# A linear attention block gated by a mixer MLP: the first step of each scale chain and its negations on VectorE instead of GpSimd, and a new table of due times

## The chip, the cores and the metric

The kernel runs on one core of one Trainium2 chip. The metric is the device time of one execution in microseconds (us), taken as the median of several runs. TensorE, VectorE, ScalarE and GpSimd are called PE, DVE, ACT and POOL, as in the profile; PEld is the loading of weights into PE, which overlaps the matmuls, and SP issues most of the DMAs.

## The reference

All data are fp32, with S = 2048 rows, D = 512 columns, 32 heads of 16, and F = 1376.

```python
xn = layernorm(x)
q, k, v = split_heads(xn @ wqkv)
phi = lambda t: where(t > 0, t + 1, exp(t)) + 1e-6
kv = einsum("bhsd,bhse->bhde", phi(k), v)
z = einsum("bhsd->bhd", phi(k))
o = (phi(q) @ kv) / (phi(q) . z + 1e-6)
s = merge_heads(o) @ wo
h = gelu(layernorm(xn) @ w1)
x1 = xn + shift_rows_by_column_quarter(h) @ w2
h2 = gelu(layernorm(x1) @ w3) @ w4
out = x + s * silu(x1 + h2)
```

The attention has no mask, so `kv` and `z` are sums over all rows.

## The kernel before

The 2048 rows are cut into 16 tiles of 128 rows, and four of these make a block; there are four blocks. Names carry the tile or the block as a number: `x5` is a tile of rows, `kr2` the key of tile 2. A product in fp32 is made of three fp32r products: an operand is split into a rounded part (`h` at the end of its name) and a rest (`l`), the rounding on ACT, the subtraction on DVE (`rounded`). A group of three matmuls on the same operands shows as `hh`, `lh`, `hl` in the trace.

The work runs in stages. First come keys and queries from the rows, and with each finished tile of keys a gram matrix `g` of rows and keys (tiles `k`, `q`, `g`; `gram`, `query`, `key`); from block 1 on, pairs of tiles are made together with fewer products (`pair_kq`, tiles `pax`, `pbx`, `pex`). Then come the mixer's first matmul (`h`), its second (`seven`, tiles `pam`, `pbm`, `pem`), the up projection (`a`, `pa`, `pb`, `pe`) with attention between (`pas`, `pbs`, `pes`), and the down projection (`acc`, `pbd`, `ped`).

`pair_kq` and `seven` are alike. Each makes seven products for four results, and uses a PSUM bank more than once: a product is added up in the bank, ACT copies the sum out (`p1`, `p5`, `u2`) or DVE adds it to such a copy (`o`, `so`, `h_a220f`), and then further matmuls add to what still stands in the bank (`go(..., False)`). The first of these must wait until the copy has read the bank. PE can meanwhile work on other products, where the order puts some.

Statistics of the rows are made on ACT, by a sum and a sum of squares (`totals`, tile `sq` into `mv`), or on DVE (`moments`). Three functions turn them into scales. `scale_x` makes, for one to four tiles, `w` (variance times a constant plus epsilon), its power −1/2 (`rs`, function `power`), the negated scale `ns`, and from these `nm` and `mr`; `halves_x` then scales and splits the rows. `spread` does the first two steps for a block (`pu`, then `an`), and PE transposes `an` into a row (`ab`). `mixed` does it for the second layer norm (`w2`, `rs2`, `nm2`). Before the change all these small steps are on POOL, which also computes the power and issues the accumulating DMAs (`gather`).

Nothing in this order is fixed by hand. The functions only add operations to a plan, in program order, each with an engine, a duration and its operands. `Plan.emit` then orders every engine's operations: PE goes by a nominal sequence, every other operation gets a due time back from those that need it, and the one due first among the ready ones is issued. A table `SOONER` shifts due times: of each pair of numbers in it, the first names an operation by its place in the plan, and the second moves its due time ahead by that many quarters of a microsecond:

```python
for n, k in zip(table[::2], table[1::2]):
    self.ops[n].due -= .25 * k
self.backward()
```

The result is one instruction stream for each engine, in which an instruction that waits holds everything behind it.

Of the kernel before, what the change touches and what calls it, by code (L numbers as in the profile page):

```python
# [11 lines left out]
ALU = mybir.AluOpType  # L12
# [3 lines left out]
EPS = 1e-5  # L16
# [380 lines left out]
def linear_attn_gated_by_mixer(  # L397
# [20 lines left out]
    QT = 4  # L418
# [16 lines left out]
    KV = KM * KM / D  # L435
# [10 lines left out]
    pl = Plan(nc, pools, counts, ("acc", "mm"))  # L446
# [14 lines left out]
    def fixed(name, n, dt=F32):  # L461

        t = pl.new("const", name, dt, n)
        t.ap = const.tile([P, n], dt, name=name)
        return t
# [37 lines left out]
    mv1, mv2 = fixed("mv1", 2 * NT), fixed("mv2", 2 * NT)  # L503
# [24 lines left out]
    def var(mv, a, b):  # L528
        return mv.cut([(2 * i + 1, 2 * i + 2) for i in range(a, b)], b - a,
                      lambda ap: ap.rearrange("p (t k) -> p t k", k=2)[:, a:b, 1])  # L530
# [48 lines left out]
    def small(name, n):  # L579
        return pl.new("sm", name, F32, n)  # L580
# [17 lines left out]
    def scale_x(lo, n):  # L598

        r, s, m = (v[:, lo:lo + n] for v in (rs1, ns1, nm1))  # L600
        w = small(f"w{lo}", n).all
        km, kv = (1.0, 1.0) if QT <= lo < 2 * QT else (KM, KV)
        pl.ts(w, var(mv1, lo, lo + n), kv, EPS, ALU.mult, ALU.add, eng="POOL")
        power(r, w, n)
        pl.ts(s, r, -km if lo < QT else -1.0, None, ALU.mult, eng="POOL")
        pl.tt(m, means(mv1, lo, lo + n), s, ALU.mult, eng="POOL")
        if lo < QT:
            pl.ts(mr1[:, lo:lo + n], m, -1.0, None, ALU.mult, eng="POOL")
        elif km != 1.0:
            pl.ts(m, m, km, None, ALU.mult, eng="POOL")  # L610
        for i in range(lo, lo + n):
            halves_x(i)

    def spread(b):

        u, m = (an[:, (2 * b + k) * QT:(2 * b + k + 1) * QT] for k in range(2))
        p = small(f"pu{b}", QT).all
        km, kv = (1.0, 1.0) if b == 1 else (KM, KV)
        pl.ts(p, var(mv1, b * QT, b * QT + QT), kv * (1.0 + EPS), EPS * EPS, ALU.mult, ALU.add, eng="POOL")
        pl.ts(m, means(mv1, b * QT, b * QT + QT), -km, None, ALU.mult, eng="POOL")  # L620
        power(u, p, QT)
        ps = pl.new("mm", f"ab{b}", F32, 512)[:2 * QT, :P]
        pl.transpose(ps, an[:, 2 * b * QT:2 * (b + 1) * QT], ident.all)
        t = pl.new("p", f"ar{b}", F32, PIECE)[:2 * QT, :P]
        pl.act(t, ps, AF.Copy)
        for k, row in enumerate((arow, nrow)):
            dst = row[:, EDGE + b * BT:EDGE + (b + 1) * BT]
            pl.store(dst.via(lambda ap: ap.rearrange("o (j p) -> (o j) p", p=P)),
                     t.via(lambda ap, k=k: ap[k * QT:(k + 1) * QT]))
# [391 lines left out]
    def mixed(i, xv):  # L1021

        b, j = divmod(i, QT)
# [6 lines left out]
        a, z = i - QT + 1, i + 1  # L1030
        r, m = rs2[:, a:z], nm2[:, a:z]
        w = small(f"w2{b}", QT).all
        pl.ts(w, var(mv2, a, z), KV, EPS, ALU.mult, ALU.add, eng="POOL")
        power(r, w, QT)
        pl.tt(m, means(mv2, a, z), r, ALU.mult, eng="POOL")
        pl.ts(m, m, -KM, None, ALU.mult, eng="POOL")
# [627 lines left out]
    b = 2  # L1664
# [21 lines left out]
    b = 3  # L1686
# [72 lines left out]
    for b in LATE:  # L1759
# [5 lines left out]
        down_late(b, final)  # L1765

    SOONER = (
# [42 lines left out]
    )  # L1810
    pl.emit(first=6.0, lead={"p": 9.0, "w": 20.0, "ab": 10.0}, reserve={"p": 8, "w": 1, "ab": 0}, window=9.0,
            ahead=6.0, table=SOONER)
# [39 lines left out]
```

## Time and profile before

| | us |
|---|---|
| runs | 503.18, 502.1, 502.8 |
| median | 502.8 |
| profiled execution | 502.62 |
| its span | 500.9 |
| first matmul starts | 1.04 |
| last matmul starts | 496.33 |

The granted clock of PE is 1.00 over the whole span. In the rows of a timeline stand the start in us from the beginning of the span, the duration in us, the engine, the line of the program (often that of a helper), the operation, what it writes and reads, and, in brackets, how long the engine stood idle ahead of it and what ended the wait. Ends of matmuls are modelled, so what is read from them is the distance between starts. In the groups of a view by lines stand the busy time of the group, the mean of one in ns, and then the idle time of the engine before them.

### The profile page before, as it was taken

What the parts mean: (1) busy time and instruction counts of PE and PEld (TensorE: products, weight loads), DVE (VectorE), ACT (ScalarE), POOL (GpSimd) and SP (SyncE); (2) the same over time, 40 slices, a digit from 0 to 9 for tenths busy, and PEclk for the clock granted to TensorE, in tenths of its full rate; (3) what the DMA queues carried; (4) which work ended last, traced back from release to release, by engine and by line L of the source; (5) the groups of instructions that cost most, each with busy time, mean ns of one, the idle gap of its engine ahead of it and who ended that gap; (6) DMA issues with size and microseconds to landing.
All of it is one profiled execution on the core that took longest, in us unless ns stands there. A gap on an engine that the chain in (4) does not pass through costs nothing.

```text
span 500.9 us, 9569 instructions
## 1 busy us (share of the span) xinstructions
PE 495.3 (99%) x3138; PEld 442.8 (88%) x3138; DVE 430.1 (86%) x850; ACT 368.0 (73%) x826; POOL 119.2 (24%) x208
## 2 busy tenths in 40 slices
PE   9999999999999999999999999999999999999996
PEld 6788778888888897899999989999989999999996
DVE  5998888789999958999899999978899785787983
ACT  5898999968696589999977855554657676856631
POOL 1384504438930232133100022000013100000320
PEclk9999999999999999999999999999999999999999
DMA  7968994999975899989978779975648937974674
GB/s 220 328 167 233 224 289 128 214 347 284 343 201 133 221 272 276 277 200 273 371 231 220 235 214 200 303 225 178 203 145 145 283 124 246 294 225 135 117 195 131
DMA packets 84345, 113.35 MB, mean 226 GB/s; under 512 B 10024, under 2 KB 37960, under 8 KB 84296
## 3 DMA queue, kind: packets, MB, share of 16 engines
q1 hardware_dynamic: 73640, 93.35, 57.2%
q0 software_dynamic: 10656, 19.40, 23.5%
q8 instruction: 24, 0.39, 0.3%
q14 instruction: 25, 0.20, 0.1%
HBM read 72.47 MB, written 36.06 MB: 217 GB/s over the span
## 4 chain that ended last, share of the span: by engine, by line
PE 94%; ACT 3%; DMA 1%; SPq 0%; DVE 0%; issue 0%; ACTq 0%
PE acc L146 12%; PE pb L146 11%; PE g L146 9%; PE h L146 9%; PE pbd L146 6%; PE pe L146 6%; PE pbx L146 5%; PE pbs L146 5%; PE pbm L146 5%; PE ped L146 3%; PE pa L146 3%; PE pex L146 3%; PE q L146 3%; PE pem L146 2%; PE pes L146 2%; PE a L146 2%
## 5 line engine op out<-in xcount | busy, mean ns | idle before, releaser
L225 POOL DMA_DIRECT2D xo<-x1d x12 | 10.6, 1067 | 186.7 <-DVE qz L201 112.6
L225 POOL DMA_DIRECT2D o<-xnd x16 | 14.0, 885 | 39.7 <-DMA w_s<-in_w 11.9
L225 POOL DMA_DIRECT2D zacc<-ke x12 | 12.3, 1028 | 31.9 <-DVE u_2l L191 9.9
L225 POOL DMA_DIRECT2D th<-in_x x14 | 12.1, 878 | 32.0 <-DVE th L201 14.3
L168 ACT ACTIVATE th<-xo 128x512 f32<-128x512 f32 (+1 forms) x16 | 9.7, 614 | 11.1 <-DVE xo L201 10.3
L225 POOL DMA_DIRECT2D xt<-nrow x16 | 15.1, 1441 | 6.0 <-DVE wt_01l L191 3.5
L191 DVE TENSOR_TENSOR ht<-h,abc 128x512 f32<-128x512 f32 x16 | 11.1, 691 | 5.6 <-PE h L146 5.4
L168 ACT ACTIVATE ht<-ht 128x512 f32<-128x512 f32 x16 | 9.9, 628 | 4.2 <-DVE ht L191 4.0
L168 ACT ACTIVATE p<-pe 128x256 f32<-128x256 f32 x20 | 7.6, 382 | 7.2 <-PE pe L146 7.1
L168 ACT ACTIVATE p<-pb 128x256 f32<-128x256 f32 x20 | 7.7, 383 | 7.2 <-PE pb L146 7.1
L196 POOL TENSOR_SCALAR w<-mv 128x4 f32<-128x4 f32 (+2 forms) x10 | 2.9, 289 | 40.0 <-ACT sq L168 39.7
L168 ACT ACTIVATE y<-o,nm,rs 128x512 f32<-128x512 f32 x16 | 12.0, 806 | 0.5 <-POOL nm L196 0.5
L168 ACT ACTIVATE u<-pb 128x256 f32<-128x256 f32 x20 | 7.7, 383 | 5.9 <-PE pb L146 5.8
L201 DVE SCALAR_TENSOR_TENSOR th<-th,so 128x512 f32<-128x512 f32 (+1 forms) x17 | 11.1, 652 | 0.8 <-ACT th L168 0.4
L168 ACT ACTIVATE sq<-o,mv 128x512 f32<-128x512 f32 x16 | 11.4, 719 | 0.1
L201 DVE SCALAR_TENSOR_TENSOR pq<-pq,rd 128x512 f32<-128x512 f32 x16 | 10.9, 682 | 0.3
L168 ACT ACTIVATE den<-den 128x32 f32<-128x32 f32 x16 | 3.6, 228 | 9.8 <-DVE den L1421 9.8
L201 DVE SCALAR_TENSOR_TENSOR qz<-pq,zb 128x512 f32<-128x512 f32 x16 | 10.8, 680 | 0.0
L168 ACT ACTIVATE gf<-gf 128x256 f32<-128x256 f32 (+1 forms) x20 | 10.5, 523 | 0.3
L1421 DVE TENSOR_REDUCE den<-qz 128x32 f32<-128x512 f32 x16 | 10.7, 676 | 0.1
L168 ACT ACTIVATE sq<-o 128x512 f32<-128x512 f32 x16 | 10.1, 630 | 0.1
L596 POOL TENSOR_TENSOR rs<-w,nhalf 128x4 f32<-128x4 f32 (+2 forms) x10 | 9.6, 962 | 0.7
(1974 smaller groups left out, 2383.5 us busy)
## 6 DMA issues: line engine op xcount, KB each, us to landing
w_s<-in_w SPq DMA_DIRECT2D x28, 256.0 KB, 5.8
x<-in_x SPq DMA_DIRECT2D x16, 256.0 KB, 5.1
xt<-in_xt SPq DMA_DIRECT2D x16, 256.0 KB, 5.7
xnd<-x SPq DMA_DIRECT2D x16, 256.0 KB, 6.0
xt<-nrow POOLq DMA_DIRECT2D x16, 256.0 KB, 8.2
pqd<-qr SPq DMA_DIRECT2D x16, 256.0 KB, 3.3
o<-xnd POOLq DMA_DIRECT2D x16, 256.0 KB, 6.0
x1d<-o SPq DMA_DIRECT2D x16, 256.0 KB, 5.8
```

The source lines that it names most:

```text
L146: lambda: nc.tensor.matmul(out.get(), lhs.get(), rhs.get(), start=start, stop=stop, skip_group_check=more))
L168: nc.scalar.activation(out.get(), src.get(), func, scale=get(scale), **kw)
L191: self.vec(eng, out, [a, b], lambda: self.e(eng).tensor_tensor(out.get(), a.get(), b.get(), op=op), True)
L196: lambda: self.e(eng).tensor_scalar(out.get(), a.get(), get(s1), get(s2), **kw), False,
L201: lambda: self.nc.vector.scalar_tensor_tensor(out.get(), a.get(), get(s), b.get(), op0=op0, op1=op1),
L225: lambda: self.nc.gpsimd.dma_start(out.get(), get(src), accum_op=ALU.add), mb=mb)
L596: lambda: g.tensor_tensor(out.get(), src.get(), nh.get(), op=ALU.pow))
L1421: pl.add("DVE", .6, .68, [t], [den], lambda: nc.vector.tensor_reduce(den.get(), t.get().rearrange("p (h d) -> p h d", d=DH), axis=AX.X, op ...
```

## The change

Four calls lose their `eng="POOL"`, so that DVE executes them: `w` and `ns` in `scale_x` (six of each), `pu` in `spread` (four) and `w` in `mixed` (four), twenty instructions in all. The power and the steps that follow from it stay on POOL.

```diff
@@ scale_x
-        pl.ts(w, var(mv1, lo, lo + n), kv, EPS, ALU.mult, ALU.add, eng="POOL")
+        pl.ts(w, var(mv1, lo, lo + n), kv, EPS, ALU.mult, ALU.add)
         power(r, w, n)
-        pl.ts(s, r, -km if lo < QT else -1.0, None, ALU.mult, eng="POOL")
+        pl.ts(s, r, -km if lo < QT else -1.0, None, ALU.mult)
@@ spread
-        pl.ts(p, var(mv1, b * QT, b * QT + QT), kv * (1.0 + EPS), EPS * EPS, ALU.mult, ALU.add, eng="POOL")
+        pl.ts(p, var(mv1, b * QT, b * QT + QT), kv * (1.0 + EPS), EPS * EPS, ALU.mult, ALU.add)
@@ mixed
-        pl.ts(w, var(mv2, a, z), KV, EPS, ALU.mult, ALU.add, eng="POOL")
+        pl.ts(w, var(mv2, a, z), KV, EPS, ALU.mult, ALU.add)
@@ the table of due times
     SOONER = (
-        15, 27, 20, 21, 26, 2, 30, 3, 36, 10, 52, 1, 82, 2, 91, 2, 99, 4, 103, 12, 112, -14, 113, -2, 124, 10,
...
+        10, 31, 24, 16, 26, 19, 28, 6, 72, 6, 91, 2, 95, 6, 97, 47, 100, 39, 117, 4, 124, 10, 133, 4, 138, 15,
...
     )
```

The table is replaced by a longer one, so the order of every engine is another. The matmuls are the same, and so are the DMAs. Three places follow; the number at the end of a name is that of a buffer.

PE, in `pair_kq` of block 1 at 58 us of the profile, from the last matmul into the bank `pex` ahead of its copy to the first behind it. Before:

```order
L146 MATMUL pex_788<-kq_t11h,xs_0l 128x512
L146 MATMUL pbx_719<-kq_t21h,xs_1h 128x512
L146 MATMUL pbx_719<-kq_t21l,xs_1h 128x512
L146 MATMUL pbx_719<-kq_t21h,xs_1l 128x512
L146 MATMUL pex_788<-wq_2h,xs_3h 128x512
L146 MATMUL pex_788<-wq_2l,xs_3h 128x512
```

Now (the last matmul into `pex` ahead of the copy, of `kq_t11h` and `xs_0l`, stands two rows ahead of these):

```order
L146 MATMUL pax_797<-wk_2l,u_2h 128x512
L146 MATMUL pax_797<-wk_2h,u_2l 128x512
L146 MATMUL pax_797<-wk_3h,u_3h 128x512
L146 MATMUL pax_797<-wk_3l,u_3h 128x512
L146 MATMUL pax_797<-wk_3h,u_3l 128x512
L146 MATMUL pbx_756<-kq_t20h,xs_1h 128x512
L146 MATMUL pbx_756<-kq_t20l,xs_1h 128x512
L146 MATMUL pbx_756<-kq_t20h,xs_1l 128x512
L146 MATMUL pbx_756<-kq_t21h,xs_1h 128x512
L146 MATMUL pbx_756<-kq_t21l,xs_1h 128x512
L146 MATMUL pbx_756<-kq_t21h,xs_1l 128x512
L146 MATMUL pex_779<-wq_2h,xs_3h 128x512
```

Where the three matmuls of one `pbx` group stood between the two, a whole `pax` group of six and two `pbx` groups stand now.

PE in the up projection at 388 us, from the last matmul into the bank `pb_1` ahead of DVE's `h_a220f` to the first behind it. Before (that last one, of `yt32h` and `w_1_s1l`, stands just ahead):

```order
L146 MATMUL pas_5536<-m_b21h,q12h 128x256
L146 MATMUL pas_5536<-m_b21l,q12h 128x256
L146 MATMUL pas_5536<-m_b21h,q12l 128x256
L146 MATMUL pas_5536<-m_b21h,q12h 128x256
L146 MATMUL pas_5536<-m_b21l,q12h 128x256
L146 MATMUL pas_5536<-m_b21h,q12l 128x256
L146 MATMUL pb_1_5429<-yt42h,w_1_b 128x256
```

Now:

```order
L146 MATMUL pb_1_5444<-yt32h,w_1_s1l 128x256
L146 MATMUL pas_5526<-m_b21l,q12h 128x256
L146 MATMUL pas_5526<-m_b21h,q12l 128x256
L146 MATMUL pas_5526<-m_b21h,q12h 128x256
L146 MATMUL pas_5526<-m_b21l,q12h 128x256
L146 MATMUL pe_1_5461<-yb222h,w_1_s1l 128x256
L146 MATMUL pe_1_5461<-yb222h,w_1_s1h 128x256
L146 MATMUL pe_1_5461<-yb222l,w_1_s1h 128x256
L146 MATMUL pe_1_5461<-yb222h,w_1_s1l 128x256
L146 MATMUL pas_5526<-m_b21h,q12l 128x256
L146 MATMUL pb_1_5444<-yt42h,w_1_b 128x256
```

The six matmuls into `pas` are five, with four into `pe_1` among them.

DVE at 22 to 26 us, where the scales of tiles 1 to 3 are made (`kt` is a step of the keys, `BN_STATS` a statistic of block 1, `wq_0l` and its like the rests of weights). Before:

```order
L201 SCALAR_TENSOR_TENSOR kt_320<-wneg,mv_90,k_145 128x512
L191 TENSOR_TENSOR wq_0l<-wq_s_157,wq_0h 128x512
L201 SCALAR_TENSOR_TENSOR kt_335<-wneg,mv_90,k_147 128x512
L191 TENSOR_TENSOR wq_3l<-wq_s_176,wq_3h 128x512
L191 TENSOR_TENSOR wq_1l<-wq_s_153,wq_1h 128x512
L201 SCALAR_TENSOR_TENSOR kt_358<-wneg,mv_90,k_165 128x512
L584 BN_STATS st_369<-x_234 128x6
L584 BN_STATS st_374<-x_240 128x6
L584 BN_STATS st_382<-x_254 128x6
L584 BN_STATS st_392<-x_264 128x6
```

Now:

```order
L201 SCALAR_TENSOR_TENSOR kt_320<-wneg,mv_90,k_155 128x512
L201 SCALAR_TENSOR_TENSOR kt_327<-wneg,mv_90,k_145 128x512
L191 TENSOR_TENSOR wq_0l<-wq_s_160,wq_0h 128x512
L196 TENSOR_SCALAR w_343<-mv_90 128x2
L584 BN_STATS st_346<-x_210 128x6
L196 TENSOR_SCALAR w_355<-mv_90 128x1
L191 TENSOR_TENSOR wq_2l<-wq_s_173,wq_2h 128x512
L196 TENSOR_SCALAR ns_94<-rs_92 128x2
L201 SCALAR_TENSOR_TENSOR kt_366<-wneg,mv_90,k_165 128x512
L196 TENSOR_SCALAR ns_94<-rs_92 128x1
L196 TENSOR_SCALAR x_197<-x_197,rs_92,nm_95 128x512
```

The two `w` and the two `ns` stand among the corrections `kt` and the rests of the weights, and three of the four statistics have gone further back.

99 rows, old and new, of the table SOONER are left out of this document.

## The prediction

> **What bounds the kernel now.** I read the page first, then the table of stretches, then the list of what the weight loads wait for, then the rows around each hole that this list names.
>
> From the page (busy time and share of each engine; the chain that ended last):
>
> ```profile
> PE 495.3 (99%) x3138; PEld 442.8 (88%) x3138; DVE 430.1 (86%) x850; ACT 368.0 (73%) x826; POOL 119.2 (24%) x208
> PE 94%; ACT 3%; DMA 1%; SPq 0%; DVE 0%; issue 0%; ACTq 0%
> ```
>
> From the view by stretches (PE, PEld, DVE, ACT, POOL busy, then the granted clock):
>
> ```profile
> 60.00:70.00 10.00, 10.00 (x45) 8.00 (x44) 8.17 (x16) 10.00 (x19) 1.10 (x2) 1.00 1.02 243
> 495.00:501.00 6.00, 1.61 (x14) 1.41 (x12) 2.58 (x6) 0.73 (x2) 0.00 (x0) 1.00 0.24 87
> ```
>
> TensorE sets the end: 94% of the chain, at full clock. POOL, which loses work, is busy for 24% of the span and absent from the chain; DVE, which gains it, is at 86%. So neither the relief of POOL nor the load on DVE is the question. It is whether TensorE has holes, and whether the new order closes or opens some. The page's 99% hides them, because a waiting matmul is drawn longer.
>
> A hole shows in the distance from one start to the next. Timeline around 58 us:
>
> ```profile
> 57.76 0.39 PE L146 MATMUL pex<-kq_t11h,xs_0l 128*128 128x512 f32 x1
> 58.19 0.69 ACT L168 ACTIVATE p5x<-pex,ns 128x512 f32<-128x512 f32 x1
> 58.23 0.39 PE L146 MATMUL pbx<-kq_t21l,xs_1h 128*128 128x512 f32 x1
> 58.46 0.40 PE L146 MATMUL pbx<-kq_t21h,xs_1l 128*128 128x512 f32 x1
> 58.93 0.50 PE L146 MATMUL pex<-wq_2h,xs_3h 128*128 128x512 f32 x1
> 59.27 0.39 PE L146 MATMUL pex<-wq_2l,xs_3h 128*128 128x512 f32 x1
> ```
>
> Unhindered, 512-column matmuls start every 0.23 us (58.23 to 58.46). Here two steps are 0.47 and 0.34, so 0.24 + 0.11 = 0.35 us is lost. The reason is a bank that is used again: the matmul at 58.93 adds into the bank that ACT is still copying to p5x, which it began after the matmul of 57.76 and ended at 58.88. Only three matmuls (0.70 us) stand between, against 0.69 of copy. I call this a loop: last matmul into a bank, copy, next matmul into the bank; its cover is the TensorE work put between. I measured the excess over 0.23 (512 columns) and 0.117 (256) of every step: about 2.4 us in all behind the first matmuls, of which some 0.6 at the very start and the larger rest in a few loops. **No order can gain more than about 2.4 us**, and the change leaves every matmul in.
>
> **The change part by part.** *The loops whose cover grows.* Beside the one above (3 matmuls before, 12 after: −0.35) these are it. Weight loads in the m products that waited, and the first of their holes:
>
> ```profile
> 191.13 0.19 PEld L146 LDWEIGHTS pbm<-w_t2h,hs21h 128*128 128x128 f32 x1 [0.44 <-ACT p1m L168]
> 193.40 0.19 PEld L146 LDWEIGHTS pbm<-w_t3h,hs31h 128*128 128x128 f32 x1 [0.45 <-ACT u2m L168]
> 195.01 0.19 PEld L146 LDWEIGHTS pbm<-w_t4h,ha221h 128*128 128x128 f32 x1 [0.48 <-DVE o L191]
> 191.13 0.50 PE L146 MATMUL pbm<-w_t2h,hs21h 128*128 128x256 f32 x1
> 191.47 0.28 PE L146 MATMUL pbm<-w_t2l,hs21h 128*128 128x256 f32 x1
> 191.59 0.28 PE L146 MATMUL pbm<-w_t2h,hs21l 128*128 128x256 f32 x1
> ```
>
> 191.13 to 191.47 is 0.34, where 191.47 to 191.59 is 0.12: 0.22 lost. The other two, stepped the same way, lose 0.22 and 0.18. Cover less copy was 0.47, 0.47 and 0.43 us there; in the new order it is 0.64, 2.00 and 0.66. Together −0.62.
>
> ```profile
> 216.28 0.27 PE L146 MATMUL pbm<-w_t3h,hs32l 128*128 128x256 f32 x1
> 216.52 0.39 PE L146 MATMUL pem<-w_b22h,hs42h 128*128 128x256 f32 x1
> 216.75 0.28 PE L146 MATMUL pem<-w_b22l,hs42h 128*128 128x256 f32 x1
> ...
> 217.34 0.36 PE L146 MATMUL pbm<-w_t4h,ha222h 128*128 128x256 f32 x1
> 217.54 0.28 PE L146 MATMUL pbm<-w_t4l,ha222h 128*128 128x256 f32 x1
> ```
>
> Two steps of 0.24 and 0.23 for 0.12 each (0.23 lost), and 0.20 at 217.34 (0.08). These two loops go from 6 to 10 and from 6 to 8 matmuls of cover: −0.31.
>
> ```profile
> 354.18 0.28 PE L146 MATMUL pb<-yb111h,w_ah 128*128 128x256 f32 x1
> 354.43 0.19 PEld L146 LDWEIGHTS pbs<-m_t4h,q 128*128 128x128 f32 x1 [0.18 <-DVE so L191]
> 354.65 0.28 PE L146 MATMUL pbs<-m_t4l,q 128*128 128x256 f32 x1
> ...
> 387.12 0.28 PE L146 MATMUL pb<-yt32h,w_s1l 128*128 128x256 f32 x1
> 387.66 0.42 DVE L191 TENSOR_TENSOR h_a220f<-pb,p 128x256 f32<-128x256 f32 x1
> 387.83 0.28 PE L146 MATMUL pas<-m_b21h,q12l 128*128 128x256 f32 x1
> 388.14 0.38 PE L146 MATMUL pb<-yt42h,w_b 128*128 128x256 f32 x1
> 388.36 0.28 PE L146 MATMUL pb<-yt42l,w_b 128*128 128x256 f32 x1
> ```
>
> At 354 two steps lose 0.24, and one matmul more (7 to 8) gives 0.12, just the 0.13 of its first step: −0.24, to 0 if that tenth does not do. At 388 the steps 387.83 to 388.14 to 388.36 are 0.31 and 0.22: 0.29 lost. Here DVE frees the bank, late; cover goes from 6 matmuls to 9, three steps or 0.35 us more: −0.29. Sum of the gains: 0.35 + 0.62 + 0.31 + 0.24 + 0.29 = **1.81 us**.
>
> *The loops whose cover shrinks.* With matmul counts times 0.117 and the copies' own durations of before, cover less copy falls in pbm, w_t4h with ha222h (one product earlier than at 217), from 0.68 to 0.32; in pem, w_b22h with hs43h, from 0.68 to 0.33; in pb, w_s1h with yt32h, from 0.32 to 0.20. What 0.32 costs, the old rows tell twice: 0.23 at 216.52, and 0.03 here (383.09 less 382.94 less 0.12):
>
> ```profile
> 382.94 0.31 PE L146 MATMUL pb<-yt32h,w_s1h 128*128 128x256 f32 x1
> 383.09 0.28 PE L146 MATMUL pb<-yt32l,w_s1h 128*128 128x256 f32 x1
> ```
>
> I take the middle, 0.13, for each of the first two, and 0.15 for the third (0.12 less cover than in these rows): **+0.41**, between 0.1 and 0.7.
>
> *The first gram.* The new order puts k2h behind three cq and an ar on ACT, and in front of k3h:
>
> ```profile
> 31.61 0.62 ACT L168 ACTIVATE k2h<-kr 128x512 fp32r<-128x512 f32 x1
> 32.39 0.27 ACT L168 ACTIVATE ar<-ab 8x128 f32<-8x128 f32 x1 [0.16 <-PE ab L151]
> 32.56 1.93 ACT L168 ACTIVATE cq<-qneg,mr 128x512 f32<-128x512 f32 x3
> ```
>
> k2h moves later by 1.93 + 0.27 − 0.62 = 1.6 us less what ACT did sooner (wait before ar 0.16, rounding of wq moved), to an end near 33.5; counted in steps, TensorE wants it at 33.35. The first product of x1h and k1h is asked for eight places earlier than before, and is about as close. I take **+0.3** for both, between 0 and 0.6. The first loads are issued in another order too (two pieces of xt ahead of a piece of wk); **+0.1** for that, between −0.5 and +0.5, the size of the holes at the start.
>
> *The twenty moved instructions.* On POOL they are these (and `w` shapes of one and two columns at about the same price); the nearest DVE operation is the BATCH_NORM_AGGREGATE, of a two-column output:
>
> ```profile
> L196 POOL TENSOR_SCALAR w<-mv 128x4 f32<-128x4 f32 x7 | 1.8, 258 | 27.7 <-ACT sq L168 27.4
> L196 POOL TENSOR_SCALAR ns<-rs 128x4 f32<-128x4 f32 x3 | 3.4, 1122 | 0.1
> 28.54 0.38 DVE L585 BATCH_NORM_AGGREGATE mv<-st 128x2 f32<-128x6 f32 x4
> 24.02 1.26 POOL L596 TENSOR_TENSOR rs<-w,nhalf 128x2 f32<-128x2 f32 x2
> ```
>
> Four aggregates fill 0.38, so 0.10 each is the floor; POOL's 0.26 is the ceiling. Twenty make 1.9 to 5.2 us of DVE in 501, and I take the floor, as it is DVE's own row. None lies on the chain: DVE has 14% free. I cost them at nothing. Without that cover each would cost its 0.1 to 0.26 once, in a stretch where ACT and TensorE have no slack (60 to 70 above). What could cost more is waiting: DVE works in order, `w` waits for ACT's square sums and `ns` for POOL's power in the last row, 1.26 for two. The new order puts a statistic or a weight rounding between `w` and `ns`, which I take as cover enough: 0.
>
> [...]
>
> *Sum.* −1.81 + 0.41 + 0.3 + 0.1 + 0 = −1.0. Against the profiled execution's 502.62 (span 500.9 and 1.7 around it) that is **501.6**; the median of the runs shown is 502.8, 0.2 above, so 501.8 by that. The tail after the last matmul (the 495 to 501 row: TensorE 1.61 of 6.00) keeps its operations, and I cost it at nothing, up to +0.1. I forecast 501.7.
>
> **The rivals.** A measurement of this kernel tells about 0.2%, 1.0 us, from no change.
>
> *The moved waits eat the gain.* Around 24 us DVE stands at `ns` until POOL's two powers are through: 1.26, and behind it are the k products' corrections, which the first gram waits for. Then −1.81 + 0.41 + 0.3 + 0.1 + 1.26 = +0.3, **502.9**: no change. For it: ACT's rows from 31.61 on leave no more than 0.16 between its operations. Against: before, POOL did the whole chain in its own time, and DVE still waits for nothing more than it did, if the operation between is long enough (0.6). [...]
>
> *Thin loops break in numbers: slower.* The new order still has 46 loops with under 0.5 us of cover less copy (before: 52, of which eight, at 0.2 each, made 1.6 of the 1.81). Whether such a loop stalls depends on one operation of DVE or ACT, 0.4 to 0.7 us in the rows above, standing in front of the copy, as at 387.66, where DVE comes 0.26 after the matmul's end at 387.40. If twelve of the 46 meet one, they cost 12 × 0.23 = 2.8, and 502.62 − 1.81 + 0.4 + 2.8 = **504.0**. It decides from about eleven on; eight of 52 in the old order speaks against, that all engines' orders were drawn anew speaks for.
>
> *The reorder does less than the counts say:* the queue in front of the copies moves with the matmuls, half of the 1.81 comes, and the costs stay: −0.9 + 0.8 = −0.1, **502.5**.
>
> **How the numbers follow.** Forecast 0.44 (all of it faster by over 0.2%, though narrowly), moved waits 0.16 and half the gain 0.18 (both within 0.2%), thin loops 0.22 (slower). The best case, every gain and no cost, is 500.8, with 0.3 for a luckier start 500.5; upward the range takes in the slower rival: 500.5 to 504.2. The forecast's own range is 500.7 to 502.2. Faster 0.44, same 0.34, slower 0.22.
>
> **What would show it.** Right: even steps of 0.23 where pex reuses its bank near 59, of 0.117 at the pbm, pem, pbs and pb places near 191 to 195, 217, 354 and 388; the wait list without p5x, p1m and u2m. Costs: a step over 0.3 at the first k2h product near 33, and near 222 (pem, hs43h) and 382 (pb, yt32h). Moved waits: DVE `ns` rows with idle time released by POOL's power. Wrong altogether, if the new trace's excess over the steps is above 2.4 us, or if TensorE's last start moves and the excess does not.

## The result, and the profile after

The changed kernel takes 504.49 us (median of nine executions, 503.58 to 505.73), the kernel before in the same round 502.8 (nine, 502.1 to 504.64). The ratio is 1.0035, with a 95% interval of 1.0023 to 1.0046: slower, by 1.2 to 2.3 us, where 1.0 faster was forecast. The profiled execution has 503.89 us and a span of 502.2, against 502.62 and 500.9.

The page of the changed kernel, busy time of the engines and the chain that ended last:

```profile
PE 495.8 (99%) x3138; PEld 442.4 (88%) x3138; DVE 432.2 (86%) x870; ACT 366.9 (73%) x826; POOL 118.8 (24%) x188
PE 96%; DMA 1%; DVE 1%; SPq 1%; ACT 0%; issue 0%
```

The twenty instructions are on DVE (870 for 850) and cost it 2 us that nobody misses. TensorE still ends the kernel. What moved is its last matmul, from 496.33 to 497.60, and it had moved before the body began. The timeline of TensorE at the start, kernel before:

```profile
8.03 0.40 PE L146 MATMUL k<-wk_0h,u_0l 128*128 128x512 f32 x1
8.48 0.49 PE L146 MATMUL k<-wk_1h,u_1h 128*128 128x512 f32 x1
8.90 0.51 PE L146 MATMUL k<-wk_1l,u_1h 128*128 128x512 f32 x1
...
13.11 1.02 PE L146 MATMUL ksum<-wkt,ones 128*128 128x512 f32 x2
```

The same of the changed kernel:

```profile
8.38 0.39 PE L146 MATMUL k<-wk_0h,u_0l 128*128 128x512 f32 x1
9.28 0.49 PE L146 MATMUL k<-wk_1h,u_1h 128*128 128x512 f32 x1 [0.51 <-ACT wk_1h L168]
10.00 0.50 PE L146 MATMUL k<-wk_1l,u_1h 128*128 128x512 f32 x1 [0.23 <-DVE wk_1l L191]
...
14.28 1.02 PE L146 MATMUL ksum<-wkt,ones 128*128 128x512 f32 x2
```

With a usual step of 0.23, the first product of the second chunk loses 0.90 − 0.23 = 0.67 us where it lost 0.22, and the next 0.49 where it lost 0.19. `ksum`, which closes this part, starts 1.17 late. From there to the last matmul it is 483.32 us, against 483.22: the whole body, where the forecast saw 1.1 us of gain, is 0.1 slower.

The chain of waits says who is late. Columns: start, length, what. Kernel before, then the changed one:

```profile
2.17 0.43 SPq L207
2.61 0.04 issue
2.65 4.82 DMA wk_s<-in_wqkv
...
7.49 0.64 ACT wk_1h L168
```

```profile
3.60 4.97 DMA wk_s<-in_wqkv
...
8.59 0.69 DVE wkt L191
9.29 0.67 DVE wk_1l L191
```

SP issues one load each 0.47 us. The second chunk of `wk` went from the fifth place (2.65) to the seventh (3.60), took as long as before to land (4.82, 4.97), and is there 1.1 us later. Nothing on this chain has slack in these two executions.

In the body I again added up what each step has above the usual one for its shape (0.232 us for 512 columns, 0.118 for 256). Over all matmuls this excess went from 9.97 to 11.39 us with the usual steps taken from each trace, and to 11.24 with those of the kernel before. That is the 1.27 us by which the last matmul moved, and it must be: the matmuls are the same, so the steps add up to the last start. What the excess tells is where the time went. The first 20 us went from 5.54 to 6.35, less than the 1.17 of the start, since a wait of 0.34 at `qsum` (at 18.6 us in the kernel before) went; behind 20 us another 0.45 was lost. By stretches of 10 us, before and after: 50 to 60, 0.42 and 0.08; 190 to 200, 1.60 and 1.58; 210 to 220, 0.36 and 0.17; 350 to 360, 0.28 and 0.03; 380 to 390, 0.39 and 0.39; and, new, 220 to 240 from 0.07 to 0.57, 300 to 310 from 0.04 to 0.48, 330 to 340 from 0.04 to 0.53. The loops named in the forecast mostly closed, and as much opened elsewhere. Two of the new holes in the changed kernel's timeline:

```profile
237.22 0.28 PE L146 MATMUL pb<-yb110h,w_ah 128*128 128x256 f32 x1
237.34 0.28 PE L146 MATMUL pb<-yb110l,w_ah 128*128 128x256 f32 x1
237.61 0.39 PE L146 MATMUL pb<-yt30h,w_s1h 128*128 128x256 f32 x1
237.84 0.29 PE L146 MATMUL pb<-yt30l,w_s1h 128*128 128x256 f32 x1
...
335.00 0.28 PE L146 MATMUL pes<-m_t1l,q6s0h 128*128 128x256 f32 x1
335.53 0.39 PE L146 MATMUL pbs<-m_b11h,q6l 128*128 128x256 f32 x1 [0.24 <-DVE q6l L191]
```

At 237.61 a bank's copy on ACT (`u`, 237.20 to 237.56) is late, 0.15 + 0.11 us; at 335.53 a rest that DVE finishes at 335.47, 0.40 us.

### The profile page after: what moved, and what is told of

Read it like the earlier page. It is cut to its first block, busy times and chain, and to the rows that moved or that the text cites. A ratio compares the mean times of both kernels' runs of the same rounds, so it can differ in the third digit from the quotient of the medians.

```text
span 502.2 us, 9571 instructions
## 1 busy us (share of the span) xinstructions
PE 495.8 (99%) x3138; PEld 442.4 (88%) x3138; DVE 432.2 (86%) x870; ACT 366.9 (73%) x826; POOL 118.8 (24%) x188
## 4 chain that ended last, share of the span: by engine, by line
PE 96%; DMA 1%; DVE 1%; SPq 1%; ACT 0%; issue 0%
PE acc L146 12%; PE pb L146 11%; PE g L146 9%; PE h L146 9%; PE pbd L146 6%; PE pe L146 6%; PE pbx L146 6%; PE pbs L146 5%; PE pbm L146 5%; PE q L146 3%; PE ped L146 3%; PE k L146 3%; PE pa L146 3%; PE pex L146 3%; PE pem L146 2%; PE a L146 2%
## 5 line engine op out<-in xcount | busy, mean ns | idle before, releaser
L225 POOL DMA_DIRECT2D zacc<-ke x12 | 10.8, 901 | 26.9 <-DMA zacc<-ke 10.2
L168 ACT ACTIVATE gf<-gf 128x512 f32<-128x512 f32 (+1 forms) x20 | 10.5, 523 | 0.5
L168 ACT ACTIVATE x<-x,nm,rs 128x512 f32<-128x512 f32 x12 | 9.5, 807 | 0.0
L168 ACT ACTIVATE so<-pbs 128x256 f32<-128x256 f32 x8 | 3.1, 384 | 8.6 <-PE pbs L146 8.5
```

The source lines that it names most:

```text
L168: nc.scalar.activation(out.get(), src.get(), func, scale=get(scale), **kw)
L225: lambda: self.nc.gpsimd.dma_start(out.get(), get(src), accum_op=ALU.add), mb=mb)
```

## The experiments

To split the change, the order that the planner had found was written out: every kernel below issues its operations in a fixed list, and what differs between two of them is a piece of that list.

```diff
-    SOONER = ( ... )
-    pl.emit(... )
+    LINE = ( ... )    # every operation, in the order in which it is issued
+    pl.emit(LINE)
```

**Four kernels, buffers chosen anew.** `start_old`: the changed kernel, with the old order up to `ksum`. `start_new`: the kernel before, with the new order up to `ksum`. `move_only`: the old order, the twenty instructions on DVE. `pool_again`: the new order, the twenty on POOL. In each, the planner gave tiles their buffers by the new order of issue.

> The changed kernel, with the instructions up to the sum of the key weights (ksum, the first 14 us) on all engines in the order of the kernel before, and the changed order from there on. Theory A, the new load order at the start costs 1.2 us (ksum starts at 14.28 instead of 13.11): ksum near 13.1, and a median about 1.2 us under the changed kernel's 504.5, so near 503.3. Theory B, the time is lost in the moved instructions or in new holes after 200 us: near 504.5 as before, within 0.3.

> The kernel before, with the instructions up to ksum in the changed kernel's order, and all twenty small instructions still on GpSimd. Theory A: ksum near 14.3 and about 1.2 us slower than the kernel before, 504.0. Theory B: as the kernel before, 502.8, within 0.3.

> The kernel before in its own order, with nothing but the twenty small instructions moved to VectorE, each placed ahead of the first VectorE instruction that began after its input was ready. Theory A: no difference, 502.8 within 0.3. Theory W, VectorE waiting for the power on GpSimd at the negations delays the gram stage: about 1.3 us slower, 504.1.

> The changed kernel's order, with the twenty small instructions back on GpSimd. Theory A: no better than the changed kernel, 504.5 within 0.3, since the order at the start stays. Theory W: the loss goes, 503.2 or less.

| kernel | us | ratio to before | 95% interval |
|---|---|---|---|
| `start_old` | 509.27 | 1.0121 | 1.0092 to 1.0150 |
| `start_new` | 508.5 | 1.0110 | 1.0088 to 1.0131 |
| `move_only` | 506.01 | 1.0064 | 1.0043 to 1.0084 |
| `pool_again` | 510.9 | 1.0160 | 1.0133 to 1.0188 |

All four lose 3 to 8 us, those that take parts back as well, so they tell nothing about the parts. With the new order of issue the tiles had got other buffers, and with them other waits. In `start_old`, by stretches (busy PE, PEld, DVE, ACT, POOL, the granted clock, DMA):

```profile
120.00:123.00 3.00, 0.00 (x0) 0.00 (x0) 2.85 (x6) 2.34 (x5) 0.23 (x1) 0.95 1.03 282
123.00:126.00 3.00, 2.85 (x7) 2.27 (x8) 3.00 (x6) 1.66 (x4) 1.55 (x3) 0.50 1.10 272
```

No matmul starts for 3 us, after DVE has waited 3.81 us (to 119.83) for the transfer `pqd<-qr`, and then the clock is halved.

**The same four, buffers as they were.** Each tile keeps the buffer that it has in the kernel from which the list comes.

```diff
+    SLOTS = ( ... )   # the buffer of each tile
-    pl.emit(LINE)
+    pl.emit(LINE, SLOTS)
```

> As start_old (the changed kernel with the old order up to ksum), but every tile keeps the buffer that it has in the changed kernel; in start_old the tiles got other buffers, too. Theory A, the load order at the start costs 1.2 us and the rest of the loss of start_old came from the buffers: ksum near 13.1, median near 503.3. Theory F, any shift of the start against the rest costs several us: above 506 again.

> The kernel before with the changed order up to ksum and its own buffers. Theory A: ksum near 14.3, median near 504.0. Theory F: above 506.

> The kernel before in its own order and with its own buffers, only the twenty small instructions on VectorE. Theory A: no difference, 502.8 within 0.4. Theory W, VectorE waits at the negations: 504.1. If the buffers were not the cause in move_only: 506 again.

> The changed kernel's order and buffers, the twenty small instructions on GpSimd. Theory A: as the changed kernel, 504.5 within 0.4. Theory W: 503.2 or less. If the buffers were not the cause in pool_again: above 508 again.

| kernel | us | ratio to before | 95% interval |
|---|---|---|---|
| `start_old2` | 502.70 | 1.0003 | 0.9992 to 1.0013 |
| `start_new2` | 503.73 | 1.0031 | 1.0017 to 1.0045 |
| `move_only2` | 502.75 | 1.0003 | 0.9992 to 1.0013 |
| `pool_again2` | 505.74 | 1.0050 | 1.0033 to 1.0067 |

Before stood at 502.46 beside them. The old start takes the loss away, the new start alone brings it, and the twenty moved instructions do nothing that can be seen. `start_old2` has the new body and is no faster than before (between 0.4 us faster and 0.7 slower). With the twenty back on POOL the new order is no better; it is even 0.8 us slower than the changed kernel by the two ratios, which was not expected. Its profiled execution (506.27) also shows the halved clock, treated below.

**Which part of the start.** `sp_only` is the changed kernel with SP's first fourteen loads in the old order; `sp_add`, the converse, is the kernel before with these in the new order; `wk1_swap` is the kernel before with one exchange. SP's loads five to nine:

```diff
  sp_add, against the kernel before
-    wk_1, xt_1, wk_2, xt_2, wk_3
+    xt_1, xt_2, wk_1, wk_2, wk_3
  wk1_swap, against the kernel before
-    wk_1, xt_1, wk_2, xt_2, wk_3
+    xt_1, wk_1, wk_2, xt_2, wk_3
```

The new order of the fourteen has two more exchanges, of the halves of `wk_0` (first and third) and of two pieces of `xt` (twelfth and thirteenth); `sp_add` has them too and `sp_only` takes them back. `wk1_swap` has the one exchange alone.

> The changed kernel with its own buffers and order, only the first fourteen loads on SP in the order of the kernel before (the second piece of key weights issued fifth instead of seventh). Theory A1, the late load of that piece alone costs the 1.2 us: ksum near 13.1 to 13.4, median near 502.7, as start_old2. Theory A2, the orders of ScalarE, VectorE and TensorE in the first 14 us carry it: ksum stays near 14.3, median stays near 504.5.

> The kernel before with two loads on SP exchanged, nothing else: the second piece of key weights is issued sixth instead of fifth, one issue or 0.47 us later. Theory A1: the first product that needs it and ksum start 0.2 to 0.5 us later, median 502.7 to 503.0. Theory A2: no difference.

> The kernel before, with one thing of the new order: the first fourteen loads on SP stand in the new order (two pieces of xt ahead of the second piece of wk), every buffer and every other engine's order as before. It is the converse of the run in which the new kernel got the old order of these loads back. Theory (the order of these fourteen loads is what delays the start): ksum starts near 14.3 us instead of 13.1, the excess over the first 20 us is near 6.3 instead of 5.5, the time is 1.0 to 1.5 us above before (503.5 to 504.4 where before stands at 502.5 to 502.9), and some of the runs show a mean granted clock of 0.994 to 0.997. Rival A (the load order costs only together with the new order of ACT, DVE and TensorE at the start): within 0.4 us of before, ksum within 0.4 of 13.1, no run with a clock below 0.998. Rival B (the loss lies past the start): within 0.4 us as well, with the start late and made up later.

`sp_only` takes 503.24 us, ratio 1.0003 (0.9989 to 1.0017); `sp_add` 503.70, ratio 1.0024 (1.0013 to 1.0034); `wk1_swap` 503.24, ratio 1.0002 (0.9988 to 1.0016). The order of fourteen loads is enough to bring the loss and to take it back. From the chain of waits of `wk1_swap` and of `sp_add`:

```profile
3.13 4.87 DMA wk_s<-in_wqkv
8.00 0.02 issue
8.03 0.63 ACT wk_1h L168
```

```profile
3.60 4.83 DMA wk_s<-in_wqkv
8.43 0.02 issue
8.45 0.63 ACT wk_1h L168
```

| | place of wk_1 on SP, issued | wk_1h starts | ksum starts |
|---|---|---|---|
| before | fifth, 2.65 | 7.49 | 13.11 |
| `wk1_swap` | sixth, 3.13 | 8.03 | 13.64 |
| `sp_add` | seventh, 3.60 | 8.45 | 14.06 |
| after | seventh, 3.60 | 8.59 | 14.28 |

In these executions each place costs its 0.47 us, in full. Not in all: in three others that issue `wk_1` fifth (`start_old2`, `move_only2`, `loops`) `wk_1h` starts at 6.75 to 6.96 and `ksum` at 12.70 to 12.86, and the chain of `start_old2` runs over TensorE alone, so a place can have some tenths of slack when the load lands early. In `wk1_swap` that half a microsecond is in the trace, but below what its interval tells (up to 0.8). `sp_only` is less clean than its time: its `ksum` starts at 13.71, since this execution's `xt_0` came late, and landings scatter by some tenths (`wk_1h`, with its load issued fifth, starts at 6.75 to 7.49).

The same traces say what the body is worth. From `ksum` to the last matmul the old body takes 482.82 to 483.23 us (before, `start_new2`, `wk1_swap`, `sp_add`), the new one 483.32 to 483.84 (after, `start_old2`, `sp_only`). The new body gains nothing in any of them.

**Closing loops by hand.** `loops` is the kernel before with ten matmuls moved, so that the loops at 58, 216, 354 and 388 get more cover: 5, 9, 9 and 9 matmuls, where the kernel before has 3, 6, 7 and 6 and the new order 12, 10, 8 and 9.

```diff
  PE's order, four places (the numbers are counts of matmuls)
+    2 more between the last matmul into pex and pex<-wq_2h,xs_3h    (58)
+    3 more ahead of pem<-w_b22h,hs42h                               (216)
+    2 more ahead of pbs<-m_t4h,q                                    (354)
+    3 more ahead of pb<-yt42h,w_b                                   (388)
```

> The kernel before with its own buffers and start, only ten matmuls on TensorE put elsewhere, ahead of the reuse of a bank: two ahead of the pex reuse at 58.9 us, three ahead of pem at 216.5, two ahead of pbs at 354.4, three ahead of pb at 388.1. If the loops are read rightly, their holes (0.35, 0.23 and part of 0.08 at 217.5, 0.24, 0.29) close: 1.1 us less, 501.4 beside 502.5 of the kernel before. If a hole only moves to the next wait: less than 0.5 us.

502.57 us, ratio 0.9991 (0.9977 to 1.0005): perhaps 0.4 us, not clear of zero. Three places of its timeline, two rows each:

```profile
218.52 0.28 PE L146 MATMUL pam<-w_b21h,ha123l 128*128 128x256 f32 x1
218.88 0.39 PE L146 MATMUL pbm<-w_t2h,hs23h 128*128 128x256 f32 x1
...
358.64 0.40 PE L146 MATMUL acc<-w_3h,f_3h 128*128 128x512 f32 x1
358.96 0.39 PE L146 MATMUL pb<-yt41h,w_b 128*128 128x256 f32 x1
...
388.59 0.28 PE L146 MATMUL pbs<-m_b11h,q12l 128*128 128x256 f32 x1
389.00 0.39 PE L146 MATMUL pes<-m_t1h,q12s0h 128*128 128x256 f32 x1
```

The places at 216, 354 and 388 step evenly now, and later ones wait instead: 0.36 − 0.12 = 0.24 at 218.88, 0.32 − 0.23 = 0.09 at 358.96, 0.41 − 0.12 = 0.29 at 389.00, and 0.1 more in the step behind each. TensorE reaches the next copy sooner than ACT does: `p1m`, which 218.88 waits for, stands behind two roundings and runs from 218.44 to 218.83. At 58 five matmuls of cover still leave 0.30 and 0.11 (before: 0.24 and 0.11), for the copy itself begins late, at 57.65, in ACT's full queue. So the four places together cost no less than before, and the body takes 482.99 us, within what the old body takes elsewhere: this trace shows no gain from the loops.

**The queue or the bytes?** Whether the late load is a matter of SP's turn or of the bytes ahead of it, four kernels ask that issue `wk_1` from ACT.

```diff
-    pl.load(self.raw[c].cols(*cs), src[:, c, cs[0]:cs[1]])
+    pl.load(self.raw[c].cols(*cs), src[:, c, cs[0]:cs[1]], eng="ACT" if name == "wk" and c == 1 else "SP")
```

`act_wk1` (from before) and `act_wk1_after` (from the changed kernel) issue it first of all on ACT; `act_wk1_late` behind ACT's roundings of `ones` and `ident`; `act_wk12` issues `wk_1` first and `wk_2` there (`c in (1, 2)`).

> The kernel before with one load moved: the second piece of wk (wk_1) is issued by ACT, ahead of all else on ACT, so near 0.8 us instead of 2.65, and every load behind it on SP stands one place sooner. Theory of the issue line (a load lands about 4.9 us after its issue): wk_1 is there near 5.7, and what the second products wait for becomes xt_1, issued near 2.65 and landing near 7.3, so ksum starts 0.3 to 0.8 us sooner than 13.1, and the time is 0.3 to 0.8 us under before. Theory of the bytes: wk_1 lands no sooner or takes its time from the first pieces of wk and xt, the first products start later by up to 1 us, and the time is equal or up to 1 us above.

> The changed kernel with that one load moved: wk_1 is issued by ACT first of all, not seventh on SP. Theory of the issue line: the hole ahead of the products of wk_1 (0.67 us) goes, ksum starts near 13.0 to 13.4 instead of 14.28, the time is 0.9 to 1.5 us under the changed kernel's 504.5, so near 503, and no run shows a mean clock below 0.998, since TensorE's hole is gone. Theory of the bytes: ksum stays within 0.3 us of 14.28, the time within 0.4 us of 504.5, and the low clocks stay.

> The kernel before with two loads moved to ACT: wk_1 ahead of all else, wk_2 behind the roundings of ones and ident, near 2.6 us instead of 3.6; SP's other loads stand one and two places sooner. Theory of the issue line: the third products are ready sooner too, and it gains what the run with one load gains and up to 0.4 us more. Theory of the bytes: no more than the run with one load, or a loss of up to 1 us.

> The kernel before with wk_1 issued by ACT behind the roundings of ones and ident, near 2.6 us, the instant at which SP issued it; only the loads behind it on SP stand one place (0.47 us) sooner. Theory of the issue line: the pair of wk_1 and xt_1 is complete with wk_1, as before, so ksum moves by 0.2 at most, later products wait less, 0 to 0.4 us gained. Theory of the bytes: within 0.2 us of before.

`act_wk1` takes 503.70 us, ratio 1.0014 (1.0000 to 1.0027), `act_wk1_after` 503.72, ratio 1.0011 (0.9997 to 1.0026). The chain of waits of `act_wk1`:

```profile
1.24 4.06 DMA xt<-in_xt
5.30 0.14 issue
5.44 8.69 PE k L146 x28
```

`wk_1` is in time (its rounding starts at 6.36, and its products step by 0.23), but the first piece of `xt`, issued at 1.24 as before, now takes 4.06 us where in the kernel before it took 2.39 (landed at 3.63), and TensorE resumes at 5.44 where before it did at 4.19. `ksum` starts at 14.43. So the theory of the issue line alone falls: the bytes put ahead went with 1.67 us more for the piece behind them, and what the second chunk wins the first loses. The clock takes part in it: TensorE starts these kernels at about half speed (last section), in the kernel before until 6.09, here until 8.74, so its first products are not only later but slower for longer. In `act_wk1_after` it is until 10.38, and `ksum` starts at 15.14. That execution (504.71) is one of the slower half; by the two ratios, 1.0011 for 1.0035, the changed kernel gains some 1.2 us, with intervals that just touch, and no execution shows a low mean clock. So neither theory's numbers hold in full there.

The other two, 508.06 us (1.0102, 1.0087 to 1.0117) and 508.15 (1.0108, 1.0094 to 1.0122), did not try what they were meant to. The load behind ACT's roundings did not go out near 2.6 but at 9.40 and 8.20, when, by the chain, a load that SP had issued at 3.59 and 3.60 had landed (at 9.38 and 8.18); ACT's other roundings stood behind it. The reason is in the traces: the loads of both engines signal eight semaphores in turn, and a load waits until the one eight places ahead of it has landed (in the kernel before, SP's seventh at 8.53, and the fifteenth goes out at 8.54). In the turn ACT's load is sixteenth and fifteenth, and shares the semaphore of SP's eighth and seventh, the very loads of 3.59 and 3.60.

## Why the prediction was wrong

**The frame held.** TensorE ended the kernel (96% of the chain), with POOL's relief and DVE's load beside the point. That the excess over even steps moved with TensorE's last start is no more proof, as the two are one sum.

**Two steps failed, each for about half of the miss.** The first is the last of the first gram's paragraph: "The first loads are issued in another order too (two pieces of xt ahead of a piece of wk); +0.1 for that, between −0.5 and +0.5, the size of the holes at the start." It cost 1.17 us up to `ksum` in the trace, and 1.2 to 1.6 by the ratios of `sp_add` and `start_new2`. Its size was taken from TensorE's holes, which say how late each load was in the old order, not how late a load will be that is put back. The rows for that were in the profile of before: SP's rows 0.47 apart, ACT idle until `wk_1` landed, `wk_1h` straight ahead of TensorE's product. Two places are 0.95 us, with no slack behind them in that execution. With +1.2 in place of +0.1 the same sum gives 502.8; with the body at +0.1 in place of −1.1 as well, 504.0.

**The second: the gains of 1.81 did not come to the end.** The loops at 58, 216 and 354 closed, for 0.35, 0.2 and 0.25; the one at 388 closed and one at 383.12 opened, for 0.29 each. The 0.62 near 191 to 195 was misread. Timelines, before and after:

```profile
195.91 0.40 PE L146 MATMUL h<-u_0h,w_0h 128*128 128x512 f32 x1
196.14 1.02 PE L146 MATMUL m<-wo_s,kvt 128*128 128x512 f32 x2
196.59 0.80 PE L146 MATMUL h<-u_0h,w_0h 128*128 128x512 f32 x1
197.23 0.39 PE L146 MATMUL h<-u_0l,w_0h 128*128 128x512 f32 x1
```

```profile
194.24 1.02 PE L146 MATMUL m<-wo_s,kvt 128*128 128x512 f32 x2
194.70 0.68 PE L146 MATMUL pbm<-w_t4h,ha221h 128*128 128x256 f32 x1
195.22 0.28 PE L146 MATMUL pbm<-w_t4l,ha221h 128*128 128x256 f32 x1
195.33 0.28 PE L146 MATMUL pbm<-w_t4h,ha221l 128*128 128x256 f32 x1
```

The product `m` is left in fp32 and not split; it shows as two matmuls, 0.46 us in all, and behind them 0.40 is lost. It is lost in one step at 196.59 to 197.23, with no bank reused (0.64 for 0.23), and at 194.70 to 195.22 in the new order (0.52 for 0.12), or in two: in the old order the product at 191.13 starts 0.18 late and the next loses 0.22. From the first start of an `m`, without the product that follows, it is 0.85 to 0.86 us in all eight cases, four in each kernel. The matmul that reused a bank at 191.13, 193.40 and 195.01 in the old order stood behind such an `m`, and its hole was the fixed price of that neighbour. More cover moves it to another step, and the ceiling of 2.4 us for any order was too high by these 0.62.

**The costs of 0.41 and 0.3.** `pbm`, w_t4h with ha222h, cost 0.10 at 214.88, and `pem`, hs43h, 0.28 at 228.61, for 0.13 each; the third shrunk loop cost nothing. The first gram's 0.3 did not come (30 to 40: 0.09 and 0.05).

**What was not in the sum:** the new holes, 0.26 at 237, 0.29 at 306, 0.51 at 335 and 0.29 at 383, 1.35 us in all. That is the rival of thin loops, in part: three of them are such loops (237, 306, 383), but not twelve, and what they cost was made up by the loops that closed. Its 504.0 is near the result by accident, as the start made the loss. `loops` shows why a sum of holes can be too good in another order: three of the four holes, closed alone, came back at a later wait.

**The moved instructions** cost nothing, as predicted (`move_only2`, 1.0003). Each takes more than the floor of 0.10 us; groups of the changed kernel's line 196 (least, median and most ns):

```profile
L196 DVE TENSOR_SCALAR w<-mv x10: 145/163/172, 13.9 to 246.2; 128x4 f32<-128x4 f32 x7, 128x1 f32<-128x1 f32 x2, 128x2 f32<-128x2 f32 x1
L196 DVE TENSOR_SCALAR ns<-rs x6: 146/161/166, 15.2 to 85.4; 128x4 f32<-128x4 f32 x3, 128x1 f32<-128x1 f32 x2, 128x2 f32<-128x2 f32 x1
```

DVE waits for POOL's power 0.5 us in all, one time, so the rival of the moved waits did not happen.

**What remains** between that 504.0 and the 504.49 goes with the clock, as far as it can be seen. Three of the nine executions had a mean granted clock under 0.997 and took 504.86 to 505.73; the other six, 503.58 to 504.72, have a median of 504.18. No trace of the changed kernel shows a fall of the clock ahead of the last matmul, as its profiled execution had none there; the last section shows one in another kernel.

Of all versions `loops` comes lowest, and its interval holds 1; none here beats the kernel before for certain.

## What to carry to other kernels

When an order is changed, price the first loads by their place in the issuing queue and by what lands on the chain of waits, before any hole in the body: where the start has no slack, a place is its full issue time (0.47 us here). Holes in a full pipeline were not independent here (`loops` closed three, and later waits took 0.24, 0.09 and 0.29 back), so a closed one is a gain only if the later waits on the same engine have room; an excess beside a matmul of another kind may be that matmul's own price (0.85 to 0.86 us at each `m`). Compare single traces by stretches that end at a common instruction, here from `ksum` on: that separates the start, which scatters, from the body. To split a reordering, keep the buffers fixed, or what is measured is the new allocation (3.1 to 5.9 us here).

## What the hardware showed unexpectedly

**The clock of the first microseconds is not what the profile prints.** The view by stretches prints a granted clock of 1.00 from the start of the span on, for the kernel before too. The steps say otherwise. Two rows of `act_wk12`:

```profile
13.72 0.63 PE L146 MATMUL k<-wk_0h,u_0h 128*128 128x512 f32 x1
14.14 0.63 PE L146 MATMUL k<-wk_0l,u_0h 128*128 128x512 f32 x1
```

That is 0.43 us for what takes 0.23 later, about half speed, under a printed clock of 1.00. The record of the clock in the traces has no entry before full speed, which begins at 15.92 in this one; nothing recorded is printed as 1.00. In `act_wk1` it begins at 8.74, in `act_wk1_after` at 10.38, in the others at 4.8 to 7.2 (before 6.09, after 6.82). In the kernel before TensorE works without a wait from 1.04 until full speed, 5.05 us, and in the changed one 5.78. The three named wait in between (`act_wk1` 1.04 us to 5.44, `act_wk1_after` 0.95 to 5.35, `act_wk12` at least 2.5 to 10.57), and full speed comes 3.30, 5.03 and 5.35 us behind the end of that wait. What sets these lengths was not shown.

**The clock falls after a hole at the start.** The profiled execution of `pool_again2` had a longer hole there than the others: 2.06 us without work, to 9.69. By stretches, the granted clock stands behind POOL's busy time:

```profile
8.00:10.00 2.00, 0.31 (x1) 0.19 (x1) 0.99 (x2) 0.99 (x3) 0.00 (x0) 1.00 0.92 326
10.00:12.00 2.00, 1.77 (x7) 1.31 (x7) 2.00 (x5) 1.93 (x5) 0.00 (x0) 0.92 0.99 291
12.00:14.00 2.00, 2.00 (x6) 1.42 (x5) 2.00 (x5) 1.73 (x7) 0.79 (x1) 0.50 0.91 298
14.00:16.00 2.00, 2.00 (x8) 1.55 (x7) 1.72 (x5) 0.00 (x0) 1.92 (x2) 0.73 0.90 298
```

At half clock this is 0.32 + 2.00 + 1.08 = 3.4 us, from 11.7 to 15.1. In `act_wk1_late`, with a hole of 4.1 us, to 9.41:

```profile
8.00:10.00 2.00, 0.59 (x1) 0.50 (x2) 0.92 (x3) 0.72 (x2) 0.00 (x0) 0.56 1.05 362
10.00:12.00 2.00, 2.00 (x4) 0.96 (x3) 0.31 (x1) 0.00 (x0) 0.00 (x0) 0.50 0.97 299
12.00:14.00 2.00, 2.00 (x6) 1.32 (x5) 1.32 (x3) 1.32 (x3) 0.00 (x0) 0.50 0.92 188
14.00:16.00 2.00, 2.00 (x8) 1.64 (x7) 2.00 (x6) 2.00 (x6) 0.00 (x0) 0.73 1.03 378
```

1.76 + 4.00 + 1.08 = 6.8 us, twice that. In `start_old` it is 0.3 + 3.0 + 0.08 = 3.4 us again, from 122.67 (clock 0.95 from 120 to 123, 0.50 to 126, 0.99 to 130), where TensorE was idle for 3.19 us to 123.15. In all 18 profiled executions these are the three falls that come while TensorE has matmuls left. The one in `pool_again2` begins 2.0 us behind the end of its hole (9.69, 11.68), the other two begin inside theirs (8.23 and 122.67). Shorter holes at the start left the clock at 1.00: 0.67 and 0.49 us in the changed kernel, 1.11 and 0.50 in `start_new2`, 1.02 in `sp_add`. So in these traces a fall goes with a hole of 2.06 us or longer, and these holes of up to 1.6 us in all went without one; how long a hole must be, and what sets the instant of the fall, was not shown.

Of the 39 executions of the four kernels with the new load order and fixed buffers (the changed kernel, `start_new2`, `pool_again2`, `sp_add`), eleven had a mean clock of 0.994 to 0.996, and took on the mean 1.0 to 2.0 us longer than the rest of their kernel (`sp_add`: 504.8 and 505.15, the others 503.18 to 503.96). Of the 60 with `wk_1` in fifth or sixth place (`start_old2`, `move_only2`, `sp_only`, `wk1_swap`, `loops`) none had, and one of the 109 of the kernel before that ran beside the experiments (504.69). A fall of 3.4 us at half clock, as in `pool_again2`, is 1.7 us of work lost, half of 3.4. So the late load seems to cost twice: its own time, and in some executions such a fall. Of these four kernels the trace shows it in `pool_again2` alone; in the others it is read from the mean clock.

**Buffers.** The same operations, in the same order on each engine, took 3.1 us more with other buffers (`move_only` against `move_only2`, by their ratios to before) to 5.9 (`start_old` against `start_old2`).
